# Attention followed by a spectral mix on one core: the mode weights loaded by transfers of four modes instead of two, into tiles of eight modes instead of four

## The chip, the cores and the metric

The kernel runs on one core of a Trainium2 chip; nothing else runs beside it. The metric is the device time of one launch in microseconds (us), the median of repeated runs. A core has five engines with an instruction queue each: TensorE (PE, matrix products; its weight loads are shown as PEld), VectorE (DVE), ScalarE (ACT), GpSimd (POOL) and SyncE (SP). Sixteen DMA engines move data between the device's memory (HBM) and the on-chip memory (SBUF, 128 partitions). An engine issues a transfer as an instruction of its own queue, and the transfer's landing is told by a semaphore.

## The reference, cut to what matters

```python
# batch 8, heads 8, seq 576, head_dim 64; 64 modes; d_model 512
scores = scale * q @ k.T, causal, plus a bias from the cumulated s       # softmax(scores) @ v
x = attention output as (8, 576, 512)
X = np.fft.rfft(x, axis=1)
Xr, Xi = real and imaginary part of X[:, :64]
Yr = einsum('bmd,mde->bme', Xr, w_r) - einsum('bmd,mde->bme', Xi, w_i)
Yi = einsum('bmd,mde->bme', Xr, w_i) + einsum('bmd,mde->bme', Xi, w_r)
y = np.fft.irfft(Y with the other modes zero, n=576, axis=1)
u = x + y
out = u + max(u @ w_ch, 0)
```

The weights `w_r` and `w_i` are 64 x 512 x 512 numbers of four bytes each, 67 MB apiece: every mode has its own matrix, and each is used once. They are read from HBM as float32 and written to SBUF as bfloat16, by a transfer that casts.

## The kernel before

**Stages.** The attention goes in 32 steps n = (g, b): four groups g of two heads (128 columns of d_model) times eight batches b. A step transposes q and k (`transposes`), forms the scores and their exponentials (`scores`, `scores4`), multiplies with v (`av`), and takes the forward transform of the step before (`fft`). When a group's eight batches are through, its 128 rows d of all weight matrices can be used. `modes(g, c)` does that for a chunk c of eight modes: sixteen products into one accumulator `yp`, four for each of (real or imaginary weights `ri`) times (even or odd row `q_`). Chunks of the groups 0 to 2 are spread over the steps by the table `mode_steps`; the group 3 comes after the last step, one chunk after another, between work on the output (`work`, `y_transposed`, `y_times_wch`, `gather`). After the last chunk the outputs are formed in the order of a list of steps written out by hand ("R0a X1 R0b F0a ..."): inverse transform, addition of x, product with `w_ch`, and the stores.

**Weights.** The list `wq` gives their order: group, chunk, `ri`, and half chunk `par`, 128 items in all. An item is a tile of four modes (`WM = 4`), 128 partitions x 4 x 512 bfloat16, 4 KB a partition. It is loaded by two transfers, one for each half h of the partitions: the lower 64 partitions hold the even modes of the chunk, the upper 64 the odd ones, and a partition holds two neighbouring rows d of a mode, so that one piece is 4 KB read and 2 KB written. A transfer thus has 64 partitions x 2 modes = 128 pieces, 512 KB read.

The first eight tiles lie in memory that is free until later (`y_acc` and the second half of `x_all`; the list `early`). The others take turns in two rings, `wpool` with `WA = 11` tiles and `wpool2` with `WB = 6`; from item `LW2 = 76` on only the first ring is used, because `wpool2` then holds products that are kept for the end (`first_product`, one tile for each of six pairs of output tiles). After the last weights, `wpool` holds the results on their way out (`result`, one tile for each pair).

**Order of the loads.** All of q, k, v and the weights are issued by POOL (L234, in `load`), in the order of the program: nothing overtakes. Before step n the kernel issues `load(...)` of q and k two by two, of v for step n + 3 (`LA = 3`), and of weights up to `on_chip[n]` tiles, the two lists merged evenly. `on_chip` is a plan made when the kernel is built: a share that grows step by step during the first eight steps, then three (later four) tiles a step, but no tile whose ring place is used by a chunk that has not been multiplied by then. After the last step the rest is issued in one go (L600), and each waits for its place. POOL has eight semaphores for its transfers in turn, so that a transfer waits for the landing of the eighth before it.

In the last chunk the sixteen products come in another order, since other work lies between the quarters:

```python
yb = modes(NG - 1, NCK - 1, {2: lambda: (first_z(0), first_z(1)), 3: first_u})
```

so that its four quarters use `ri` 0 `par` 0, `ri` 0 `par` 1, `ri` 1 `par` 0 and `ri` 1 `par` 1 in turn.

Of the kernel before, what the change touches and what calls it, by code (L numbers as in the profile page):

```python
# [11 lines left out]
BF16 = mybir.dt.bfloat16  # L12
# [6 lines left out]
def kernel(  # L19
# [12 lines left out]
    B, H, S, D = q.shape  # L32
    NM = moe_w_r.shape[0]
    DM = H * D
    P = 128
# [4 lines left out]
    NG = DM // P  # L40
# [5 lines left out]
    MC = 8  # L46
    NCK = NM // MC
    WM = 4
    WA, WB = 11, 6
    LA = 3  # L50
    NF = NT - 1
    RP = P // 4
# [6 lines left out]
    HP = P // 2  # L59
# [41 lines left out]
    y_acc = gp.tile([P, NCK, DM], FP32, name="y_acc")  # L101
# [7 lines left out]
    wpool = ctx.enter_context(tc.tile_pool(name="w_sb", bufs=WA))  # L109
    wpool2 = ctx.enter_context(tc.tile_pool(name="w2_sb", bufs=WB))  # L110
# [77 lines left out]

    wq = [
        (g, c, ri, par) for g in range(NG) for c in range(NCK) for ri in range(2) for par in range(2)
    ]
    early = [y_acc[:, c : c + 2, :].rearrange("p c e -> p (c e)").bitcast(BF16) for c in (2, 4, 6)]
    xg = x_all[:, NG // 2 :].rearrange("p g b t d -> p (g b t d)").bitcast(BF16)
    early += [xg[:, i * WM * DM : (i + 1) * WM * DM] for i in range(5)]
    early = [e.rearrange("p (m e) -> p m e", e=DM) for e in early]
    NE = len(early)
    wt = {}

    LW2 = 76

    def ring_of(k):
        if k < NE:
            return None
        return int(k < LW2 and (k - NE) % (WA + WB) >= WA)

    def loads_w(upto):
        todo = []
        while len(wt) < min(upto, len(wq)):  # L210
            g, c, ri, par = key = wq[len(wt)]
            i = ring_of(len(wt))
            if i is None:
                t = early[len(wt)]
            else:
                t = (wpool, wpool2)[i].tile([P, WM, DM], BF16, name="w_sb", tag="w")
            src = (moe_w_r, moe_w_i)[ri]
            m0 = c * MC + par * MC // 2
            for h in range(2):
                first = 1 if ri == 1 and m0 + h == 0 else 0  # L220
                todo.append((
                    t[HP * h : HP * h + HP, 2 * first :].rearrange("p (m q) e -> p m (q e)", q=2),
                    src[m0 + h + 2 * first : m0 + MC // 2 : 2, g * P : (g + 1) * P, :].rearrange(
                        "m (p q) e -> p m (q e)", q=2
                    ),
                ))
            wt[key] = t
        return todo

    def load(*lists):  # L230

        todo = [((i + 0.5) / len(l), x) for l in lists for i, x in enumerate(l)]
        for _, (dst, src) in sorted(todo, key=lambda t: t[0]):
            nc.gpsimd.dma_start(out=dst, in_=src)  # L234

    NW = 2 * MC // WM
    mode_steps = {B: [0, 1, 2, 3], B + 1: [4], B + 2: [5], B + 4: [6], B + 6: [7]}
    for c in range(NCK, (NG - 1) * NCK):  # L240
        mode_steps.setdefault(B + c - (0 < c % NCK < 4), []).append(c)
    used = [NW * sum(len(cs) for t, cs in mode_steps.items() if t < n) for n in range(N + 1)]
    W0 = 3
    on_chip = []
    for n in range(N):
        w = W0 + (WA + WB + NE - W0) * (n + 1) // (B + 1) if n < B else on_chip[-1] + (3 if n <= 2 * B else 4)

        nt, ring = 0, ([], [])
        while nt < min(w, len(wq)):
            i = ring_of(nt)  # L250
            if i is not None:
                depth = (WA, WB)[i]
                if len(ring[i]) >= depth and ring[i][-depth] >= used[n]:
                    break
                ring[i].append(nt)
            nt += 1
        on_chip.append(nt)


    nc.sync.dma_start(out=s_sb, in_=s.rearrange("b h t -> (b h) t"))  # L260
# [1 line left out]
    nc.sync.dma_start(out=negm32, in_=d_negm)  # L262
    first = loads_qk(0)
    load(first[:2])
    load(loads_w(W0), loads_v(0) + loads_tails(0) + first[2:] + loads_v(1))
# [189 lines left out]
    def modes(g, c, meanwhile=None):  # L455


        ps = auxpool.tile([P, DM], FP32, name="yp", tag="aux")
        cols = xs[g % 2].rearrange("p q k h r b m -> p q k (h r b) m")

        def product(ri, q_, cg):
            k0 = HP if ri == 1 and c == 0 and cg == 0 else 0
            nc.tensor.matmul(  # L463
                ps[32 * cg : 32 * cg + 32, :],
                cols[k0:, q_, 1 - ri, :, c * MC // 2 + cg],
                wt[(g, c, ri, cg // 2)][k0:, 2 * (cg % 2) + q_, :],
                start=(ri == 0 and q_ == 0), stop=(ri == 1 and q_ == 1),
                tile_position=(k0, 32 * cg), skip_group_check=True,
            )
# [59 lines left out]
    def first_transposed(i, x):  # L529
# [7 lines left out]
        xts1[i, x] = spool.tile([P, DT, P], FP16, name="xt1", tag="yt")  # L537
        nc.vector.tensor_copy(out=xts1[i, x], in_=ps)  # L538

    def first_product(i, x):  # L540
        if x == 0:
            t = wpool2.tile([P, WM, DM], BF16, name="z1", tag="w").rearrange("p m e -> p (m e)")
            kept_place(i, t)
        ps = auxpool.tile([P, DM], FP32, name="z1_ps", tag="aux")
        for dt in range(DT):
            nc.tensor.matmul(  # L546
                ps, xts1[i, x][:, dt, :], wch_sb[:, dt, :], start=(dt == 0), stop=(dt == DT - 1)
            )
        keep_product(i, x, ps)
# [7 lines left out]
    with tc.tile_pool(name="sc_psum", bufs=2, space=PSUM) as scpool, \  # L557
# [7 lines left out]
        for n in range(N):  # L565
# [21 lines left out]
            i = first_pairs[n - N + len(first_pairs)] if n >= N - len(first_pairs) else None  # L587
# [9 lines left out]
                first_product(i, 1)  # L597
        av(N - 1, 1)
        fft(N - 1)
    load(loads_w(len(wq)))  # L600
    at.close()


# [20 lines left out]
    places = [finpool.tile([P, 4 * DM], BF16, name="r_sb", tag="r", bufs=3) for i in range(2)]  # L624
# [35 lines left out]
    def keep(i):  # L660
        x_times_wch(i, True)
        j = late.index(i)
        if j < len(places):
            t = places[j]
        else:
            t = wpool.tile([P, WM, DM], BF16, name="z1", tag="w").rearrange("p m e -> p (m e)")
        kept_place(i, t)
        for x in range(2):
            keep_product(i, x, zs.pop((i, x)))

# [119 lines left out]
    def result(i):  # L790
        if i == 0:
            t = finpool.tile([P, 4 * DM], BF16, name="r_sb", tag="r", bufs=3)
        else:
            t = wpool.tile([P, WM, DM], BF16, name="r_w", tag="w").rearrange("p m e -> p (m e)")
        return t.bitcast(FP32).rearrange("p (x e) -> p x e", x=2)

    def relu(i, x):
# [62 lines left out]
    c = NCK - 2  # L860
# [69 lines left out]
    for step in (  # L930
# [8 lines left out]
        i = int(step[1:].rstrip("ab"))  # L939
# [34 lines left out]
```

## Time and profile before

| | |
|---|---|
| median of three runs | 443.68 us (443.49, 443.68, 444.41) |
| span of the profiled execution, first to last instruction | 441.4 us |
| mean granted TensorE clock | 0.914 |
| PE busy | 344.0 us (78%), 4409 products |
| DVE, ACT, POOL busy | 253.2, 226.2, 241.5 us |
| DMA packets of POOL's transfers | 63408, 81.29 MB written |
| HBM read, written | 163.51 MB, 9.44 MB |

The profile records one execution on its own, whose time outside the span is not recorded; the median of the runs is 2.3 us above its span. The page of the profile gives the busy time of each engine, the span in 40 slices with the busy share of engines and DMA, the transfers by queue and by line, the chain of waits followed back from the last instruction, and the costliest groups of instructions. A group's line shows what is written from what, how often, its busy time with the mean of one, and the idle time of its engine just before with what ended it. Behind the page, the trace can be asked for a timeline of an engine, a table by stretches of time, and the record of every DMA packet (start, duration, size).

### The profile page before, as it was taken

What the parts mean: (1) busy time and instruction counts of PE and PEld (TensorE: products, weight loads), DVE (VectorE), ACT (ScalarE), POOL (GpSimd) and SP (SyncE); (2) the same over time, 40 slices, a digit from 0 to 9 for tenths busy, and PEclk for the clock granted to TensorE, in tenths of its full rate; (3) what the DMA queues carried; (4) which work ended last, traced back from release to release, by engine and by line L of the source; (5) the groups of instructions that cost most, each with busy time, mean ns of one, the idle gap of its engine ahead of it and who ended that gap; (6) DMA issues with size and microseconds to landing.
All of it is one profiled execution on the core that took longest, in us unless ns stands there. A gap on an engine that the chain in (4) does not pass through costs nothing.

```text
span 441.4 us, 10806 instructions
## 1 busy us (share of the span) xinstructions
PE 344.0 (78%) x4409; PEld 207.5 (47%) x4409; DVE 253.2 (57%) x574; ACT 226.2 (51%) x421; POOL 241.5 (55%) x381
## 2 busy tenths in 40 slices
PE   1688998898686978792956658989987887787994
PEld 1455656465354545460634325655554445442341
DVE  7766775676545546471643515766655443451795
ACT  1486788267545725571543324666650424420794
POOL 7766566565565655555655555555544444440293
PEclk9998999999969889896786967999998988998999
DMA  9999999999999999999999999999999999998498
GB/s 180 201 206 206 204 206 205 207 207 206 209 199 207 205 208 207 207 207 208 202 206 206 208 207 203 208 205 206 200 209 211 209 210 209 210 213 163 154 383 343
DMA packets 72768, 93.25 MB, mean 211 GB/s; under 512 B 29760, under 2 KB 31296, under 8 KB 72720
## 3 DMA queue, kind: packets, MB, share of 16 engines
q0 software_dynamic: 63408, 81.29, 105.0%
q1 hardware_dynamic: 9312, 11.29, 7.7%
q8 instruction: 34, 0.56, 0.5%
q14 instruction: 14, 0.11, 0.1%
HBM read 163.51 MB, written 9.44 MB: 392 GB/s over the span
## 4 chain that ended last, share of the span: by engine, by line
DMA 53%; PE 24%; DVE 12%; issue 5%; ACT 3%; POOL 2%; DVEq 0%; ACTq 0%; POOLq 0%
DMA w_sb<-in_moe_w_i_dram 31%; DMA w_sb<-in_moe_w_r_dram 20%; PE yp L463 3%; PE sc_ps L382 3%; PE z_ps L655 3%; DMA qk<-in_k_dram 2%; PE u_ps L781 2%; DVE qt L344 2%; PE sc_ps L376 2%; POOL w_sb L234 2%; PE u_ps L751 2%; DVE xs L453 2%; PE av_ps L418 2%; PE tr_ps L340 2%; DVE xt L538 1%
## 5 line engine op out<-in xcount | busy, mean ns | idle before, releaser
L390 ACT ACTIVATE p_sb<-sc_ps,cumt_sb 128x576 f16<-128x576 f32 (+1 forms) x256 | 141.9, 636 | 22.2 <-PE sc_ps L382 21.8
L234 POOL DMA_DIRECT2D w_sb<-in_moe_w_r_dram x120 | 71.1, 594 | 59.1 <-DMA w_sb<-in_moe_w_i_dram 18.1
L234 POOL DMA_DIRECT2D w_sb<-in_moe_w_i_dram x120 | 70.9, 593 | 55.0 <-DMA w_sb<-in_moe_w_i_dram 20.2
L382 PE MATMUL sc_ps<-qt,kt 128*128 128x512 bf16 (+2 forms) x384 | 78.3, 317 | 8.2 <-ACT kt L344 7.5
L344 DVE COPY qt<-tr_ps 64x576 bf16<-64x576 bf16 x64 | 47.8, 746 | 52.5 <-PE tr_ps L340 52.5
L234 POOL DMA_DIRECT2D v<-in_v_dram x72 | 52.0, 722 | 41.3 <-DMA w_sb<-in_moe_w_r_dram 10.7
L340 PE MATMUL tr_ps<-ident,qk 64*64 64x64 bf16 x1152 | 34.6, 205 | 43.9 <-DMA qk<-in_k_dram 15.0
L382 PEld LDWEIGHTS <-kt 128*128 128x128 bf16 x384 | 38.7, 106 | 37.2 <-ACT kt L344 14.7
L340 PEld LDWEIGHTS <-qk 64*64 64x64 bf16 x1152 | 26.5, 117 | 60.7 <-DVE kt L344 19.0
L376 PE MATMUL sc_ps<-negm,ident 128*128 128x256 bf16 x256 | 54.2, 297 | 0.2
L463 PE MATMUL yp<-w_sb,xs 128*32 128x512 bf16 (+1 forms) x480 | 42.0, 415 | 15.2 <-DMA w_sb<-in_moe_w_i_dram 13.6
L361 ACT ACTIVATE p<-sc_ps,cumt 128x64 f16<-128x64 f32 x32 | 10.1, 314 | 78.0 <-PE sc_ps L357 77.8
L418 PE MATMUL av_ps<-v,p_sb 128*128 128x65 f16 x1024 | 44.3, 197 | 1.2 <-DVE x_all L428 0.5
L344 ACT COPY kt<-tr_ps 64x576 bf16<-64x576 bf16 x32 | 22.9, 715 | 37.7 <-DVE qt L344 37.2
L418 PEld LDWEIGHTS <-p_sb 128*128 128x128 f16 x1024 | 37.8, 100 | 8.4 <-DVE x_all L428 3.4
L453 DVE CAST xs<-ft_ps 64x128 bf16<-64x128 f32 x128 | 36.6, 286 | 7.2 <-PE ft_ps L443 5.8
L423 DVE TENSOR_REDUCE den<-av_ps 128x5 f32<-128x10 f32 x64 | 10.8, 169 | 50.3 <-PE av_ps L418 49.3
L463 PEld LDWEIGHTS <-xs 128*32 128x32 bf16 (+1 forms) x512 | 18.9, 145 | 32.2 <-DMA w_sb<-in_moe_w_i_dram 14.0
L428 DVE TENSOR_TENSOR x_all<-av_ps,rcp 128x320 f16<-128x320 f32 x64 | 31.5, 492 | 2.2
L524 ACT COPY z<-z_ps 128x512 f32<-128x512 f32 x22 | 12.9, 586 | 26.7 <-PE z_ps L546 14.1
L443 PE MATMUL ft_ps<-Ff_sb,x_all 128*64 128x192 f16 (+1 forms) x320 | 24.1, 264 | 1.0 <-DVE x_all L428 1.0
L344 DVE COPY kt<-tr_ps 64x576 bf16<-64x576 bf16 x32 | 24.4, 762 | 0.4
(108 smaller groups left out, 432.9 us busy)
## 6 DMA issues: line engine op xcount, KB each, us to landing
w_sb<-in_moe_w_r_dram POOLq DMA_DIRECT2D x120, 256.0 KB, 8.5
w_sb<-in_moe_w_i_dram POOLq DMA_DIRECT2D x117, 256.0 KB, 9.1
out_dram<-r_w SPq DMA_DIRECT2D x16, 512.0 KB, 3.0
v<-in_v_dram POOLq DMA_DIRECT2D x72, 64.0 KB, 7.4
qk<-in_q_dram POOLq DMA_DIRECT2D x15, 288.0 KB, 8.0
qk<-in_k_dram POOLq DMA_DIRECT2D x15, 288.0 KB, 9.1
x_all<-in_moe_w_i_dram POOLq DMA_DIRECT2D x6, 256.0 KB, 7.7
y_acc<-in_moe_w_r_dram POOLq DMA_DIRECT2D x4, 256.0 KB, 7.9
```

What stands on the lines that cost most here:

```text
L234: nc.gpsimd.dma_start(out=dst, in_=src)
L340: nc.tensor.transpose(ps[rows, r, :], src[rows, r, :], ident16[rows, rows])
L344: copy(out=to[:, :, :, half * RH : half * RH + RH], in_=ps[HP * i : HP * i + HP].rearrange("d r (h p) -> d h p r", h=2),)
L376: nc.tensor.matmul(ps[:, bass.ds(w * S, W)], ident16, negm[:, bass.ts(r, W)], start=True, stop=False, skip_group_check=True,)
L382: nc.tensor.matmul(ps[:, c0 : c0 + i1 - i0], keys[:, w, r, :], qh[:, i0:i1], start=False, stop=True, skip_group_check=True,)
L390: nc.scalar.activation(out=pt[:, poff[x] : poff[x] + S - w * W], in_=ps[:, w * S : (w + 1) * S - w * W], func=ACTF.Exp, bias=cumt_sb[:, x, ...
L418: nc.tensor.matmul(ps[:, I, r : r + NCH], lhsT, rhs, start=(i == 0), stop=(i == len(todo) - 1), skip_group_check=True,)
L428: nc.vector.tensor_tensor(out=x_all[:, g, b, :, D * h : D * h + D], in0=ps[:, :, 1 : NCH], in1=rcp.unsqueeze(2).to_broadcast([P, NT, D]), ...
L443: nc.tensor.matmul(ps[HP * q_ : HP * q_ + HP].rearrange("p h f -> p (h f)"), x_all[:nT, g, b, T, q_::2], Ff_sb[:nT, T, :], start=(T == 0), ...
L453: nc.vector.tensor_copy(out=xs[g % 2][HP * h : HP * h + HP, q_, :, h, :, b, :], in_=a)
L463: nc.tensor.matmul(ps[32 * cg : 32 * cg + 32, :], cols[k0:, q_, 1 - ri, :, c * MC // 2 + cg], wt[(g, c, ri, cg // 2)][k0:, 2 * (cg % 2) + ...
L655: nc.tensor.matmul(zs[i, x], xts[i][:, x, dt, :], wch_sb[:, dt, :], start=(dt == 0), stop=(last and dt == DT - 1), skip_group_check=True,)
```

## The change

Weights are loaded by transfers of four modes a partition half (256 pieces, 1 MB read) into tiles of eight modes (`UM`, 8 KB a partition), so that a list item is now a chunk and `ri`, 64 in all. The rings have five and three such tiles (40 and 24 KB a partition, 64 KB together; before 44 and 24, 68 KB together). The first eight half tiles lie in the free memory as four units; three of these are in one piece and are loaded by two transfers, the fourth is in two places and is loaded by four. The last unit of all is also loaded by four transfers, one half chunk after the other as before. The plan still counts half tiles but deals them in twos, starts with four instead of three, and keeps an odd rest for the next step. The kept products and the results take half a tile each (`half_of`), two to a tile. The products of `modes` are the same in number, order and shape.

```diff
     WM = 4
-    WA, WB = 11, 6
+    UM = 2 * WM
+    WA, WB = 5, 3
...
-    LW2 = 76
+    LW2 = 38
...
     def loads_w(upto):
         todo = []
-        while len(wt) < min(upto, len(wq)):
-            g, c, ri, par = key = wq[len(wt)]
-            i = ring_of(len(wt))
+        while 2 * len(wt) < min(upto, 2 * len(wq)):
+            k = len(wt)
+            g, c, ri = key = wq[k]
+            i = ring_of(k)
             if i is None:
-                t = early[len(wt)]
+                halves_, t = early[k], whole[k] if k < len(whole) else None
             else:
-                t = (wpool, wpool2)[i].tile([P, WM, DM], BF16, name="w_sb", tag="w")
+                t = (wpool, wpool2)[i].tile([P, UM, DM], BF16, name="w_sb", tag="w")
+                halves_ = [t[:, x * WM : x * WM + WM] for x in range(2)]
+            if k == len(wq) - 1:
+                t = None
             src = (moe_w_r, moe_w_i)[ri]
-            m0 = c * MC + par * MC // 2
-            for h in range(2):
-                first = 1 if ri == 1 and m0 + h == 0 else 0
-                todo.append((
-                    t[HP * h : HP * h + HP, 2 * first :].rearrange("p (m q) e -> p m (q e)", q=2),
-                    src[m0 + h + 2 * first : m0 + MC // 2 : 2, g * P : (g + 1) * P, :].rearrange(
-                        "m (p q) e -> p m (q e)", q=2
-                    ),
-                ))
-            wt[key] = t
+            for m0, m1, d in [(0, MC, t)] if t is not None else [(0, WM, halves_[0]), (WM, MC, halves_[1])]:
+                for h in range(2):
+                    first = 1 if ri == 1 and c == 0 and m0 + h == 0 else 0
+                    todo.append((
+                        d[HP * h : HP * h + HP, 2 * first :].rearrange("p (m q) e -> p m (q e)", q=2),
+                        src[
+                            c * MC + m0 + h + 2 * first : c * MC + m1 : 2, g * P : (g + 1) * P, :
+                        ].rearrange("m (p q) e -> p m (q e)", q=2),
+                    ))
+            wt[key] = halves_
...
-    W0 = 3
+    W0 = 2
...
-        w = W0 + (WA + WB + NE - W0) * (n + 1) // (B + 1) if n < B else on_chip[-1] + (3 if n <= 2 * B else 4)
+        w = 4 + 2 * (WA + WB + NE - 2) * (n + 1) // (B + 1) if n < B else plan + (3 if n <= 2 * B else 4)
+        plan = w
...
-        on_chip.append(nt)
+        if nt < w // 2:
+            plan = 2 * nt + 1
+        on_chip.append(2 * nt)
...
-                wt[(g, c, ri, cg // 2)][k0:, 2 * (cg % 2) + q_, :],
+                wt[(g, c, ri)][cg // 2][k0:, 2 * (cg % 2) + q_, :],
...
+    def half_of(pool, name):
+
+        t = open_unit.pop(name, None)
+        if t is not None:
+            return t[:, HU:]
+        t = pool.tile([P, UM, DM], BF16, name=name, tag="w").rearrange("p m e -> p (m e)")
+        open_unit[name] = t
+        return t[:, :HU]
+
     def first_product(i, x):
         if x == 0:
-            t = wpool2.tile([P, WM, DM], BF16, name="z1", tag="w").rearrange("p m e -> p (m e)")
-            kept_place(i, t)
+            kept_place(i, half_of(wpool2, "z1"))
...
         if i == 0:
             t = finpool.tile([P, 4 * DM], BF16, name="r_sb", tag="r", bufs=3)
         else:
-            t = wpool.tile([P, WM, DM], BF16, name="r_w", tag="w").rearrange("p m e -> p (m e)")
+            t = half_of(wpool, "r_w")
```

The numbers of tiles on chip by the plan, counted in half tiles of four modes, before and after: at step 3 both 12, at step 8 25 and 24, at step 16 49 and 48, at step 24 81 and 80, at step 25 85 and 82, at step 26 87 and 86, at step 31 103 and 102.

More of the change, by code (lines that the diff above doesn't have):

```diff
@@ L187, in loads_tails @@
         ]
[L191 to L194, printed above, removed]
+    wq = [(g, c, ri) for g in range(NG) for c in range(NCK) for ri in range(2)]
+    ya = y_acc.rearrange("p c e -> p (c e)").bitcast(BF16)
     xg = x_all[:, NG // 2 :].rearrange("p g b t d -> p (g b t d)").bitcast(BF16)
-    early += [xg[:, i * WM * DM : (i + 1) * WM * DM] for i in range(5)]
-    early = [e.rearrange("p (m e) -> p m e", e=DM) for e in early]
+    HU = WM * DM
+    early = [[xg[:, i * HU : i * HU + HU] for i in (0, 1)], [ya[:, i * HU : i * HU + HU] for i in (1, 2)]]
+    early += [[xg[:, i * HU : i * HU + HU] for i in (2, 3)], [ya[:, 3 * HU :], xg[:, 4 * HU : 5 * HU]]]
     NE = len(early)
+    early = [[e.rearrange("p (m e) -> p m e", e=DM) for e in pair] for pair in early]
+    whole = [xg[:, : 2 * HU], ya[:, HU : 3 * HU], xg[:, 2 * HU : 4 * HU]]
+    whole = [e.rearrange("p (m e) -> p m e", e=DM) for e in whole]
     wt = {}
-    LW2 = 76
+    LW2 = 38
     def ring_of(k):
@@ L234, in load @@
             nc.gpsimd.dma_start(out=dst, in_=src)
-    NW = 2 * MC // WM
+    NW = 2
     mode_steps = {B: [0, 1, 2, 3], B + 1: [4], B + 2: [5], B + 4: [6], B + 6: [7]}
@@ L242 @@
     used = [NW * sum(len(cs) for t, cs in mode_steps.items() if t < n) for n in range(N + 1)]
-    W0 = 3
+    W0 = 2
     on_chip = []
     for n in range(N):
-        w = W0 + (WA + WB + NE - W0) * (n + 1) // (B + 1) if n < B else on_chip[-1] + (3 if n <= 2 * B else 4)
+        w = 4 + 2 * (WA + WB + NE - 2) * (n + 1) // (B + 1) if n < B else plan + (3 if n <= 2 * B else 4)
+        plan = w
         nt, ring = 0, ([], [])
-        while nt < min(w, len(wq)):
+        while nt < min(w // 2, len(wq)):
             i = ring_of(nt)
@@ L264 @@
     load(first[:2])
-    load(loads_w(W0), loads_v(0) + loads_tails(0) + first[2:] + loads_v(1))
+    load(loads_w(2 * W0), loads_v(0) + loads_tails(0) + first[2:] + loads_v(1))
     nc.sync.dma_start(out=Ff_sb, in_=d_Ff.rearrange("(T p) c -> p T c", p=P))
@@ L538, in first_transposed @@
         nc.vector.tensor_copy(out=xts1[i, x], in_=ps)
+    open_unit = {}
+    def half_of(pool, name):
[5 more added lines that the diff above has]
+        return t[:, :HU]
     def first_product(i, x):
         if x == 0:
-            t = wpool2.tile([P, WM, DM], BF16, name="z1", tag="w").rearrange("p m e -> p (m e)")
-            kept_place(i, t)
+            kept_place(i, half_of(wpool2, "z1"))
         ps = auxpool.tile([P, DM], FP32, name="z1_ps", tag="aux")
@@ L599 @@
         fft(N - 1)
-    load(loads_w(len(wq)))
+    load(loads_w(2 * len(wq)))
     at.close()
@@ L662, in keep @@
         j = late.index(i)
[L663 to L667, printed above, removed]
+        kept_place(i, places[j])
         for x in range(2):
```

## The prediction

> **What bounds the kernel now.** The page comes first: which resource is full, and what the end hangs on.
>
> ```profile
> DMA  9999999999999999999999999999999999998498
> GB/s 180 201 206 206 204 206 205 207 207 206 209 199 207 205 208 207 207 207 208 202 206 206 208 207 203 208 205 206 200 209 211 209 210 209 210 213 163 154 383 343
> ...
> q0 software_dynamic: 63408, 81.29, 105.0%
> ...
> DMA 53%; PE 24%; DVE 12%; issue 5%; ACT 3%; POOL 2%; DVEq 0%; ACTq 0%; POOLq 0%
> ...
> L234 POOL DMA_DIRECT2D w_sb<-in_moe_w_r_dram x120 | 71.1, 594 | 59.1 <-DMA w_sb<-in_moe_w_i_dram 18.1
> ```
>
> The DMA engines are full from the first slice to slice 36, where the weights end, at an almost constant 206 GB/s written (twice that read, since weights are cast to half the size). The chain runs through weight transfers for half the span. POOL, which issues them, mostly waits for landings. So the bytes in the stream set the time until the last weights land, at 407.4 us by the landing semaphores, and the output stage of some 34 us follows.
>
> Then POOL's timeline in a stretch with nothing but weights:
>
> ```profile
> 356.62 0.59 POOL L234 DMA_DIRECT2D w_sb<-in_moe_w_r_dram  x1 [0.97 <-PE xt_ps L642]
> 357.57 0.59 POOL L234 DMA_DIRECT2D w_sb<-in_moe_w_r_dram  x1 [0.35 <-DMA w_sb<-in_moe_w_r_dram]
> 359.06 0.59 POOL L234 DMA_DIRECT2D w_sb<-in_moe_w_r_dram  x1 [0.91 <-DMA w_sb<-in_moe_w_r_dram]
> 360.07 0.59 POOL L234 DMA_DIRECT2D w_sb<-in_moe_w_r_dram  x1 [0.42 <-DMA w_sb<-in_moe_w_r_dram]
> ...
> 379.11 0.59 POOL L234 DMA_DIRECT2D w_sb<-in_moe_w_r_dram  x1 [0.90 <-DMA w_sb<-in_moe_w_r_dram]
> ```
>
> Issues keep step with landings: 18 transfers from 356.62 to 379.11, 1.25 us each. The packet records say what fills that time. One transfer puts 128/16 = 8 packets of 2 KB on each DMA engine; each starts 154 ns after the one before on its engine (the commonest spacing), and behind them stands one packet of 4 bytes, the semaphore's, 21.7 ns on average (5808 of them: 363 transfers x 16). 8 x 154 + 21.7 = 1254 ns: the spacing is explained with nothing left over.
>
> Last, PE's timeline at the end of the stream:
>
> ```profile
> 395.93 1.09 PE L463 MATMUL yp<-w_sb,xs 128*32 128x512 bf16 x16
> ...
> 401.60 1.16 PE L463 MATMUL yp<-w_sb,xs 128*32 128x512 bf16 x8
> ...
> 405.42 0.65 PE L463 MATMUL yp<-w_sb,xs 128*32 128x512 bf16 x4 [0.70 <-DMA w_sb<-in_moe_w_i_dram]
> ...
> 407.47 0.65 PE L463 MATMUL yp<-w_sb,xs 128*32 128x512 bf16 x4
> ```
>
> PE meets the last tiles with 0.70 us of waiting, and the last quarter starts when PE is through with the work before it (405.42 + 0.65 + 1.4 of L781, L751, L762), as the last transfer lands (407.43). PE and DMA are level here; a gain has to move both.
>
> **The semaphore packets.** 256 weight transfers now (by the page 120 + 117 + 6 + 4 + 4 + 3 + 1 + 1). Afterwards 62 units take two and two take four: 132. So 124 go, each with 21.7 ns on every engine: 124 x 21.7 = 2.69 us off the stream. The 2 KB packets stay, 16 in a row instead of 8. From below: if the packet runs wholly beside data, nothing is saved. The stretch excludes that, for without it eight packets would take 1232 and not 1250 ns; the spacing minus 8 x 154 gives 18, or 2.2 us in all. From above: the mean spacing over 340 to 384 us is 158 ns a packet, semaphores included; if all of 8 x 4 ns went with the transfer's end, 32 ns, 4.0 us. I take 2.69, the packet's own record.
>
> [...]
>
> **What moves PE.** Up to 354.8 us PE waits for weights chunk by chunk: chunk 2 of the last group gets its last products at 354.82, its last tile landing at 354.78. By that tile 106 of the transfers are gone: 106 x 21.7 = 2.30 us earlier. From there PE works almost without a gap until 401.60, and this block moves with its start. The next-to-last quarter waits for data: 405.37 - 2.65 = 402.7; PE is there at 404.64 - 2.3 = 402.3. The last one starts at the later of 407.43 - 2.69 = 404.7 and 402.7 + 2.05 = 404.8. So the end moves by 2.3 (PE) to 2.7 (DMA); I take 2.5. The output stage is unchanged.
>
> **Does the queue stay full?** The ring loses one half tile of 17 and places come free in twos. I compared, for every load that waits for PE, the moment its place was free with the landing of the transfer before it. Before, the smallest distances are 7.3 us (q, k at 23 us) and 9.4 us (chunk 6, second half, free at 383.51, queue busy until 392.89); else above 12 near the end. Afterwards unit k of the last stage waits for unit k - 5, both halves. The tightest is unit 61 (chunk 6, `ri` 1): it needs chunk 4's first unit, free at 383.56, and the queue then has work until unit 60 has landed, 389.86 - 2.6 = 387.3. That is 3.7 us if PE did not move at all, 6.0 if it moves by 2.3. A transfer into an idle queue costs 2.95 us beyond its own moving (the first: issued 1.24, landed 4.90, moving about 0.7). So nothing runs dry; all other units have over 10 us. At step 25 the plan sends three half tiles (7.5 us) less; the queue is over 24 us ahead there (places free at 247 to 254, busy until 278). Cost nought, covered by those distances; without cover, up to 2.95 us at one place.
>
> **Edits with one answer.** POOL: 256 pieces of v take it 722 ns, so two issues of 594 become one of about 722, over 50 us less in a queue that idles for 45%: nothing. Products need both halves of a unit at once anyway (`cg // 2` runs over both within a quarter), except in the last chunk, whose last unit stays in four transfers: nothing. At the start k of step 1 stands behind one more MB (2.5 us later); PE's first steps slip, but the queue is not fed by them: nothing at the end. Results and kept products in half tiles come back ten instead of eleven later, 9 us or more after the store that frees them, against 3.0 us for a store: nothing. SP's small loads share the engines with longer runs of weights; `qt` lands after 4.8 us now in steps of about 10: nothing, or single us of PE in steps where PE has slack.
>
> **Sum.** Profiled execution 441.4 - 2.5 = 438.9 of span; the median stands 2.3 above its span, so 443.7 - 2.5 = 441.2 us. (About 0.2%, 0.9 us, can be told from no change.)
>
> **The rivals.**
> *Longer packets (slower).* A transfer now walks four modes that lie 2 MB apart instead of two. If this lengthens the 2 KB packets, the gain is gone at 154 + 2.5/2032 = 155.2 ns (32512 packets / 16 = 2032 an engine), and each further ns costs 2.0 us. Against it: the 2 MB step is in every transfer now and the packets still run at 4096 B/154 ns = 26.6 GB/s read, on all engines alike. For it: a few packets of 220 to 294 ns stand among those of 173, and the mean is 155.3 against 154, for a reason unseen. Price: at 157 ns +6.1 - 2.5 = +3.6, 447.3 us.
> [...]
> *Gain eaten in the last chunk (no change).* The last unit's halves are now parts of one tile. If PE's third quarter waits for all four transfers, that quarter and the work behind it (0.65 + 1.4) come after the last landing: 2.5 - 2.05 = 0.45 us left, 443.2 us. Against it: the two partition halves of one tile are loaded now without one waiting for the other, and pieces of `x_all` and `y_acc` are used side by side.
> *More comes off.* From 391.13 to 407.43 eleven transfers land at 1.48 us instead of 1.25, 2.5 us lost beside SP's `yv` stores. If longer runs lose less there: up to 5 us, 438.7 us. PE, level with DMA, speaks against most of it.
>
> **How the numbers follow.** The forecast has 0.72 (own range 440.4 to 441.9 by 2.2 to 2.7 with the scatter of the three runs; 439.7 by the upper bound of 4.0), more 0.06, eaten 0.09, slower 0.13. The range from 439.8 to 443.4 takes in the eaten gain and most of the bounds, and leaves out the longer packets and the full extra gain. Faster: 0.72 + 0.06 = 0.78; same 0.09; slower 0.13.
>
> **What would show it.** Right: 132 weight transfers (239 in POOL's queue instead of 363, 1984 fewer packets of 4 bytes), 2.48 us between landings of 1 MB, 2 KB packets still 154 ns apart, DMA digits at 9 until slice 36, chunk 2's last products near 352.5, the last quarter near 404.8, the stage behind it 34 us as now. Wrong: longer packets, a DMA digit below 9 before slice 36, POOL waiting for PE in the last stage with landings over 3 us apart, or the last two quarters starting together.

## The result and the profile after

The changed kernel takes 441.92 us (median of 4 runs, 441.27 to 442.63), the kernel before beside it 443.59 us (443.42 to 444.41). The ratio is 0.9957, 95% interval 0.9945 to 0.9969: by the ratio 1.9 us faster (1.4 to 2.4), by the difference of the two medians 1.7. The forecast was 441.2 us, with a range from 439.8 to 443.4. The profiled execution is the slowest of the four, 442.63 us with a span of 440.8.

First the page after: slices of the DMA engines' busy share and of GB/s written, POOL's queue, the chain, and the two groups of weight transfers.

```profile
DMA  9999999999999999999999999999999999996498
GB/s 179 205 207 204 205 206 208 207 209 207 207 204 208 210 207 209 207 209 209 204 209 209 209 208 208 207 210 206 209 211 212 212 211 211 199 218 118 160 381 341
...
q0 software_dynamic: 61424, 81.28, 104.5%
...
DMA 52%; PE 26%; DVE 14%; issue 3%; ACT 2%; POOL 2%; DVEq 0%; POOLq 0%; ACTq 0%
...
L241 POOL DMA_DIRECT2D w_sb<-in_moe_w_i_dram x62 | 38.5, 623 | 87.5 <-PE yp L473 27.5
...
L241 POOL DMA_DIRECT2D w_sb<-in_moe_w_r_dram x60 | 37.4, 623 | 53.6 <-DMA w_sb<-in_moe_w_r_dram 33.0
```

The DMA digits stay at 9 to slice 36. The bytes are the same, with 1984 fewer packets (63408 to 61424): 124 transfers on 16 engines. The mean rate in the middle slices rises by one or two GB/s. Slice 37, where the weights run out, falls from 163 to 118.

POOL's timeline in the stretch with nothing but weights (start, duration, what, and the idle time before it with what ended it):

```profile
348.58 0.61 POOL L241 DMA_DIRECT2D w_sb<-in_moe_w_r_dram  x1 [1.62 <-DMA w_sb<-in_moe_w_r_dram]
351.31 0.61 POOL L241 DMA_DIRECT2D w_sb<-in_moe_w_i_dram  x1 [2.13 <-DMA w_sb<-in_moe_w_i_dram]
353.54 0.61 POOL L241 DMA_DIRECT2D w_sb<-in_moe_w_i_dram  x1 [1.62 <-DMA w_sb<-in_moe_w_i_dram]
...
382.31 1.22 POOL L241 DMA_DIRECT2D w_sb<-in_moe_w_i_dram  x2 [13.23 <-PE yt_ps L695]
```

One transfer moves twice as much for one issue of 0.61 us. The landings that these issues follow are 2.48 to 2.49 us apart (355.74, 358.24, 360.73, 363.21 and so on), as forecast. The 13.23 us of waiting is for unit 61's place, the spot that the forecast called the tightest. Its load was issued at 382.31, and the transfer ahead of it landed at 387.98, 5.7 us later. Yet the DMA engines were not full there (stretches of 2 us: length, busy us of PE, PEld, DVE, ACT, POOL with counts, then PE's granted clock, DMA share and GB/s):

```profile
380.00:382.00 2.00, 1.20 (x20) 0.63 (x20) 0.69 (x1) 0.59 (x1) 0.00 (x0) 1.00 1.13 212
382.00:384.00 2.00, 1.27 (x12) 0.43 (x14) 0.00 (x0) 0.59 (x1) 1.69 (x3) 1.00 0.94 167
```

A landing is told when the last of the sixteen engines is through (the issue that waits for it comes 0.28 us or more behind that); the first was through with that transfer at 382.94, 5.0 us before the last, and had nothing more to do until unit 61 came. The share falls from 1.13 to 0.94, which is 2 x 0.19/1.13 = 0.3 us of the stream.

PE's work from chunk 2 of the last group to the end of the weights. First chunk 2's last products before, in the chain that ended last (start, duration):

```profile
354.82 1.07 PE yp L463 x6
```

and the timeline of the changed kernel:

```profile
353.30 0.67 PE L473 MATMUL yp<-w_sb,xs 128*32 128x512 bf16 x8 [3.61 <-DMA w_sb<-in_moe_w_i_dram]
...
393.96 0.66 PE L473 MATMUL yp<-w_sb,xs 128*32 128x512 bf16 x8 [0.30 <-DMA w_sb<-in_moe_w_i_dram]
...
399.46 1.09 PE L473 MATMUL yp<-w_sb,xs 128*32 128x512 bf16 x8 [1.57 <-DMA w_sb<-in_moe_w_r_dram]
400.48 1.03 PE L767 MATMUL z_ps<-yv,G_sb 96*128 96x512 f16 x2
...
404.14 1.07 PE L473 MATMUL yp<-w_sb,xs 128*32 128x512 bf16 x4
...
406.79 0.65 PE L473 MATMUL yp<-w_sb,xs 128*32 128x512 bf16 x4
```

Chunk 2's last products come 1.52 us earlier than before (353.30 against 354.82), not 2.30. The last weights land at 405.46, 1.97 us earlier than before (407.43), not 2.69. And the last quarter starts at 406.79, only 0.68 us earlier: it no longer meets the landing, but comes 1.33 us behind it. The groups in between take about 1.06 us where they took 0.60. The granted clock, in the same kind of lines, tells why:

```profile
395.00:400.00 5.00, 1.97 (x16) 0.78 (x16) 1.39 (x2) 0.59 (x1) 0.00 (x0) 0.88 1.12 217
400.00:405.00 5.00, 5.00 (x24) 1.16 (x16) 0.00 (x0) 0.00 (x0) 0.00 (x0) 0.50 0.66 123
```

PE runs at half its clock over 400 to 405 us. Before, the same stretch had 0.73:

```profile
400.00:405.00 5.00, 4.71 (x24) 1.40 (x23) 0.69 (x1) 0.00 (x0) 0.00 (x0) 0.73 1.08 205
```

### The profile page after: what moved, and what is told of

Its sections match the earlier page's. It is cut to its first block, busy times and chain, and to the rows that moved or that the text cites. A ratio compares the mean times of both kernels' runs of the same rounds, so it can differ in the third digit from the quotient of the medians.

```text
span 440.8 us, 10650 instructions
## 1 busy us (share of the span) xinstructions
PE 342.5 (78%) x4409; PEld 204.5 (46%) x4409; DVE 252.9 (57%) x574; ACT 226.0 (51%) x421; POOL 171.8 (39%) x257
## 3 DMA queue, kind: packets, MB, share of 16 engines
q0 software_dynamic: 61424, 81.28, 104.5%
## 4 chain that ended last, share of the span: by engine, by line
DMA 52%; PE 26%; DVE 14%; issue 3%; ACT 2%; POOL 2%; DVEq 0%; POOLq 0%; ACTq 0%
DMA w_sb<-in_moe_w_r_dram 21%; DMA w_sb<-in_moe_w_i_dram 13%; DMA qk<-in_k_dram 8%; DMA qk<-in_q_dram 6%; DMA v<-in_v_dram 4%; PE yp L473 3%; PE sc_ps L392 3%; PE z_ps L675 3%; DVE xs L463 3%; DVE qt L354 3%; PE av_ps L428 2%; PE sc_ps L386 2%; DVE x_all L438 2%; DVE xt L548 2%; PE z_ps L767 2%
## 5 line engine op out<-in xcount | busy, mean ns | idle before, releaser
L241 POOL DMA_DIRECT2D w_sb<-in_moe_w_i_dram x62 | 38.5, 623 | 87.5 <-PE yp L473 27.5
L241 POOL DMA_DIRECT2D w_sb<-in_moe_w_r_dram x60 | 37.4, 623 | 53.6 <-DMA w_sb<-in_moe_w_r_dram 33.0
L473 PEld LDWEIGHTS <-xs 128*32 128x32 bf16 (+1 forms) x512 | 17.7, 146 | 45.9 <-DMA w_sb<-in_moe_w_i_dram 25.4
L493 DVE TENSOR_TENSOR y_acc<-yp,y_acc 128x512 f32<-128x512 f32 x16 | 11.1, 692 | 29.2 <-PE yp L473 28.5
```

The costliest lines, as they stand in the source:

```text
L473: nc.tensor.matmul(ps[32 * cg : 32 * cg + 32, :], cols[k0:, q_, 1 - ri, :, c * MC // 2 + cg], wt[(g, c, ri)][cg // 2][k0:, 2 * (cg % 2) + ...
```

## The experiments

The letters of theories in an expectation stand for what that text says of them.

**The changed kernel again** (`e1_again`, no edit), as a second trace beside the others.

> The changed kernel once more, unaltered, to see what of the 1.9 us (ratio 0.9957) is steady and what is one execution's. Theory A (the stream gains 21.7 ns for each transfer that is gone; what the end keeps of it varies by execution, since the slowest of the 16 DMA engines and PE's granted clock in the last chunk decide): ratio 0.994 to 0.996, the last weight landing in this profile again 2.0 to 2.7 us before the 407.43 of the kernel before, and the last quarter's products starting at a distance from that landing which is not the 1.3 us of the first profile. Rival B (the tiles of eight modes cost PE a fixed stretch in the last chunk): the last quarter again starts 1 us or more after the last landing.

442.12 us, ratio 0.9959 (0.9946 to 0.9972). The last weights land at 405.38, the last quarter starts at 406.14. The median span is 440.35 us against 441.70 of the kernel before, 1.35 less. What lies around the span is 1.77 against 2.07 us, so 0.3 us of the gain lie outside anything that the forecast looked at.

**Tiles, rings and plan alone** (`e2_two_modes`): every unit by four transfers of two modes.

```diff
-            for m0, m1, d in [(0, MC, t)] if t is not None else [(0, WM, halves_[0]), (WM, MC, halves_[1])]:
+            for m0, m1, d in [(0, WM, halves_[0]), (WM, MC, halves_[1])]:
```

> Tiles, rings and plan of the changed kernel, but every unit loaded by four transfers of two modes (512 KB read each), 256 weight transfers instead of 132. Theory A (only the number of transfers counts): 124 x 21.7 ns = 2.7 us back on the stream, so the time of the kernel before, ratio to it 0.999 to 1.001; packets of 4 bytes again 5808. Rival C (the gain comes from the tiles, the rings or the plan, or from fewer waits of POOL): the time of the changed kernel, ratio about 0.996.

444.41 us, ratio 1.0013 (1.0000 to 1.0026). So the number of transfers is worth 444.41 - 442.12 = 2.3 us, and the tiles, rings and plan cost about 0.6 us (0 to 1.2). The last weights land at 408.62, 1.2 us later than before, with as many semaphore packets, and 3.2 us later than in `e1_again`. Of these 3.2 us e1 loses 0.7 again: its last quarter starts 0.76 us behind the landing, that of e2 0.04 us behind it:

```profile
408.66 0.65 PE L473 MATMUL yp<-w_sb,xs 128*32 128x512 bf16 x4 [0.87 <-DMA w_sb<-in_moe_w_i_dram]
```

**One ring tile less, nothing else** (`e4_ring10`, on the kernel before).

```diff
-    WA, WB = 11, 6
+    WA, WB = 10, 6
```

> The kernel before with its first ring cut from eleven tiles to ten (64 KB of rings together, as in the change), nothing else. Theory A (the queue is over 9 us ahead of every place that comes free, a tile less costs nothing): ratio 0.999 to 1.001. Rival E (the smaller ring takes part of the gain): slower by 0.3 us or more, ratio over 1.001.

444.19 us, ratio 1.0009 (0.9996 to 1.0022); the last weights land 0.45 us later (407.88). The interval takes in no change. Nor do the 0.45 us point to the ring: a profile of a kernel with the loads and all eleven tiles of the kernel before (`e9_before_awake`, below) has the last landing at 407.77. So whether the ring has a part in the 0.6 us is not shown.

**Twice as many transfers** (`e3_one_mode`): one mode each.

```diff
-            for m0, m1, d in [(0, MC, t)] if t is not None else [(0, WM, halves_[0]), (WM, MC, halves_[1])]:
+            for m0, m1, d in [(x * 2, x * 2 + 2, halves_[x // 2][:, x % 2 * 2 : x % 2 * 2 + 2]) for x in range(4)]:
...
+                    if first:
+                        continue
```

> The same tiles, rings and plan, every unit loaded by eight transfers of one mode (256 KB read each), about 508 weight transfers. Theory A: 376 more semaphore packets on each engine than in the changed kernel, 376 x 21.7 ns = 8.2 us, so 5.5 us over the kernel before: ratio 1.012. Theory D (what counts is how many bytes eight transfers in flight hold, the stream running dry when they are few): eight transfers now hold 5 us of stream, POOL stalls of 2 to 3 us and the spread between engines empty it: ratio over 1.03. Rival C (transfers cost nothing): ratio about 0.996.

488.8 us, ratio 1.1011 (1.0982 to 1.1040). The semaphore packets account for 5.5 us of this; the rest is a stream that runs dry. From its page, the share of the DMA engines, the rate and the chain, then POOL:

```profile
DMA  9999999999999999999999999999999999999298
GB/s 181 200 172 186 177 175 165 165 173 192 200 173 191 196 176 163 190 185 199 181 195 195 159 203 186 186 171 198 184 159 200 206 196 196 203 215 166 98 362 343
...
DMA 38%; PE 24%; POOL 19%; DVE 9%; issue 8%; ACT 1%; DVEq 0%; POOLq 0%; ACTq 0%
...
L243 POOL DMA_DIRECT2D w_sb<-in_moe_w_r_dram x240 | 125.2, 533 | 41.9 <-issue 16.6
```

The digits of the DMA share stay at 9 here too, at 159 to 215 GB/s. So a 9, which the prediction named as a sign, does not tell that the queue stays full; the rate does.

In all three sizes POOL has at most eight transfers in flight, and never issues one sooner than 0.28 us after the landing of the eighth before it. Eight of this size are 8 x (4 x 154 + 21.7) = 5.1 us of stream, where the changed kernel has up to 20. Besides, an issue takes 533 ns, where the engines need 638 for the transfer. POOL has moved from 2% to 19% of the chain. Which of the two, depth or issue, costs more was not taken apart.

**The rival made true** (`e5_last_whole`): the last unit too by two transfers.

```diff
-            if k == len(wq) - 1:
-                t = None
```

> The changed kernel, but its last unit too is loaded by two transfers of eight... that is four modes a partition half, one for each half, instead of four of two modes, so that the last chunk's third quarter cannot be fed before all of it has landed. The forecast (the last quarter starts when PE is through with the third, about level with the last landing): the stream ends 2 x 21.7 ns earlier, but the third quarter starts at or behind the last landing (405.4 in the changed kernel) instead of 404.1, so the last quarter starts near 407.6 and the end comes 1 to 2 us later than in the changed kernel, 443 to 444 us. The rival (the output stage hangs on something else, and the quarter's place in the order is hidden): the same time as the changed kernel, 442.0.

444.23 us, ratio 1.0009 (0.9990 to 1.0028), 2.1 us more than the changed kernel. The third quarter comes behind the last landing (405.77):

```profile
405.82 1.08 PE L471 MATMUL yp<-w_sb,xs 128*32 128x512 bf16 x4 [1.49 <-DMA w_sb<-in_moe_w_i_dram]
409.46 0.65 PE L471 MATMUL yp<-w_sb,xs 128*32 128x512 bf16 x4
```

So without the four transfers of the last unit nothing of the gain is left at the end. The size is less firm: the twelve runs scatter from 442.57 to 447.05 us, and in this profile the third quarter and the work behind it run at half the clock, 3.64 us from its start to the last quarter's.

**The last two units by four transfers** (`e6_split_two`).

```diff
-            if k == len(wq) - 1:
+            if k >= len(wq) - 2:
                 t = None
```

> The changed kernel, but the last two units instead of the last one are loaded by four transfers of two modes each. In the changed kernel PE waits 1.57 us (0.50 in the repeated run) for the whole of the last unit but one before the last chunk's first quarter. If that wait sets the last quarter's start, which stands 0.7 to 1.4 us behind the last landing, the end comes 0.5 us earlier, ratio to the kernel before 0.9948 where the changed kernel has 0.9959. If the last landing or the work between the quarters sets it, the two further transfers cost 2 x 21.7 ns and the time is that of the changed kernel within 0.1 us.

441.02 us (five of six runs between 440.96 and 441.09), ratio 0.9939 (0.9924 to 0.9955): the fastest version. The last quarter meets the landing (405.27) again, with the clock full:

```profile
402.41 0.65 PE L473 MATMUL yp<-w_sb,xs 128*32 128x512 bf16 x4 [0.23 <-DMA w_sb<-in_moe_w_i_dram]
...
405.31 0.65 PE L473 MATMUL yp<-w_sb,xs 128*32 128x512 bf16 x4 [0.85 <-DMA w_sb<-in_moe_w_i_dram]
...
395.00:400.00 5.00, 2.44 (x16) 0.92 (x16) 1.18 (x2) 0.59 (x1) 0.00 (x0) 1.00 1.09 212
400.00:405.00 5.00, 4.23 (x25) 1.51 (x23) 0.00 (x0) 0.00 (x0) 0.00 (x0) 1.00 0.50 102
```

By the ratios it gains 0.9 us on the changed kernel, where 0.5 was expected; the two intervals overlap. PE has the first eight products of the last chunk in two parts, one of them 1.9 us earlier, and 2.44 us of work between 395 and 400 instead of 1.97.

**A small load of odd rows in every step** (`e7_odd_rows`).

```diff
+    odd = ap_.tile([P, 1021], FP32, name="odd")
...
+            nc.sync.dma_start(
+                out=odd[0:33:32, :], in_=moe_w_ch.rearrange("a e -> (a e)")[: 2 * 1024].rearrange("(a e) -> a e", a=2)[:, :1021]
+            )
```

> The changed kernel with a further small load of two rows of 1021 fp32 elements in each of the 32 steps, which nothing uses. If such a row goes to few of the sixteen DMA engines and always the same, those engines get 64 further packets of 4 KB, some 154 ns each by the rate of the weight packets: 9.9 us on one engine or 4.9 on each of two, but only 0.6 us on the mean of sixteen. Theory S (a transfer lands with its slowest engine, and the slowest engine's queue sets the end of the stream): the last landing and the end come 4 to 10 us later, 446 to 452 us, and the spread between the first and the last engine of one transfer grows by as much. Theory M (the mean over the engines sets the end, fast engines wait for none): 0.6 us later, 442.7. If the rows are spread over all engines, or the queue lets a fast engine run on no further than eight transfers ahead, it lies between.

443.84 us, ratio 0.9997 (0.9986 to 1.0008), between the two theories. At 340 and 380 us the stream is 0.7 to 1.0 us behind the two profiles of the changed kernel at equal work, and the sixteen engines' landings of one transfer lie 6.4 instead of 5.0 us apart. That spread grew by 1.4 us and not by the 9.9 of one engine, so the rows did not all go to one, and this tells little. The last two experiments come back to the question, for the stores.

**PE kept awake** (`e8_pe_awake`; the kernel before likewise in `e9_before_awake`, without the first addition; with the last two units split in `e10_split_awake`, with 3 in place of 7).

```diff
+        if meanwhile:
+            for x in range(7):
+                nc.tensor.matmul(ps, ident16h, wch_sb[:, x % DT, :], start=True, stop=True)
...
+        if c == NCK:
+            for x in range(4 * DT):
+                nc.tensor.transpose(ps[:, x % DT, :], ident16h, ident16h)
...
+        if c == NCK - 2:
+            for x in range(3):
+                nc.tensor.matmul(vp, ident16h, wch_sb[:, x, :], start=True, stop=True)
```

> The changed kernel with idle time of TensorE before the last chunk filled by work that is thrown away: 16 transposes of the identity ahead of chunk 6's transposes, 3 products ahead of its product with the channel weights, 7 ahead of the last chunk's first quarter. In the changed kernel the granted clock is 0.50 from 398.9 to 405.3 us (0.50 from 397.0 to 403.4 in the repeated run), the products there take 1.06 instead of 0.60 us, and the last quarter starts 0.8 to 1.3 us behind the last landing (0.76 in the repeated run). Theory C (the clock falls because PE was idle too long, and the slow clock is what keeps the last quarter from the landing): clock 1.00 there, last quarter within 0.1 us of the last landing, the end 0.7 to 1.3 us earlier, 441.0 us, ratio 0.994, and less scatter. Rival (PE's order and waits set the last quarter, the clock falls for another reason): the same clock or the same distance, 442.1, or later by what the added work takes.

> The kernel before with the 16 transposes and 3 products of the same kind at the same places, none ahead of the last chunk. Before, the clock is 0.50 for 3 us (399.4 to 402.7) and the last quarter starts at 407.47, 0.04 us behind the last landing. Theory C: nothing is to be had there, since the landing sets the end; ratio 1.000 within 0.001. If the clock itself cost time before too, it would gain as e8_pe_awake does, 0.997.

> The changed kernel with its last two units loaded by four transfers each and the same work thrown away (3 products ahead of the last chunk instead of 7). With four transfers each alone five of six runs lay at 441.0 and one, with a lower clock, at 442.3. Theory C: all runs at 441.0, ratio 0.994; the two measures do not add, since the last landing then sets the end in both. If the waits for whole units cost time besides the clock, it is below e8_pe_awake by some tenths.

443.00 (ratio 0.9977, 0.9967 to 0.9986), 445.38 (1.0035, 1.0021 to 1.0048) and 442.64 us (0.9971, 0.9959 to 0.9982): all three slower than expected, by 1.6 to 2.0 us. PE did what was expected in all three: the clock is 1.00 over the whole last chunk and the last quarter starts 0.04 to 0.05 us behind the landing. In `e8_pe_awake` (landing 405.39):

```profile
397.98 1.67 PE L472 MATMUL yp<-wch_sb,ident16h 128*128 128x512 f16 x7
399.58 0.67 PE L476 MATMUL yp<-w_sb,xs 128*32 128x512 bf16 x8
...
405.44 0.65 PE L476 MATMUL yp<-w_sb,xs 128*32 128x512 bf16 x4 [0.88 <-DMA w_sb<-in_moe_w_i_dram]
```

There PE's last product starts 1.36 us earlier than in the changed kernel's profile (433.44 against 434.80), but the last store lands at 439.92 against 439.74. Fifteen engines are done with that store at 438.40, the sixteenth 1.52 us later. In the trace a packet of 16 KB of queue q8, "instruction" on the page, starts at 428.65 and takes 1.51 us. From the next landing on, one engine is that much behind, and it stays so: the landings that follow are 1.2 to 1.3 us apart (the two half-size stores at the end about 0.65), and at each the sixteenth engine is 1.4 to 1.7 us behind the fifteenth. In `e9_before_awake` and `e10_split_awake` such a packet comes at 433.64 and 430.21, and the sixteenth engine is 1.61 and 1.27 us late at the last store. In the changed kernel, its repeat and the kernel with the last two units split, the last such packet came at 408.7 to 410.2 us.

**The added instructions without the work, and the work without the packet's place.** `e12_code_only` is the changed kernel with 26 one-column products thrown away far ahead of the end; `e11_awake_code` is `e8_pe_awake` with 96 of them (condition `h == 0 or r == 0`).

```diff
+            if h == 0 and r == 0 and n < 26:
+                nc.tensor.matmul(ps[:, :1], ident16, negm[:, :1], start=True, stop=True)
```

> The kernel with TensorE kept awake (16 transposes and 3 + 7 products thrown away), and besides 96 products of a single column, three in each of the 32 steps, thrown away too. In the run without them the clock was 1.00 throughout and the last quarter met the landing (405.44 against 405.39), yet the time was 443.0: a 16 KB packet of an instruction queue, which came at 408.7 us in the kernel with the split units, came at 428.65, among the result's stores, and from then on the last of the sixteen engines landed each store 1.5 us behind the fifteenth (439.92 against 438.40 at the last store). These packets come every 256 of TensorE's instructions or so, and 52 more brought one into the stores. With 192 further ones ahead of it the packet should fall near 409 us again, where no store is under way. Theory S (the end waits for the engine that carried that packet): the stores' engines land together again, 441.0 to 441.4 us, ratio 0.994. Rival (the added work on TensorE itself costs the 1.5 us): 443 or more.

> The changed kernel with 26 products of a single column, one in each of the first 26 steps, thrown away: 52 instructions for TensorE as in the kernel that was kept awake, and nothing else. Theory S: the 16 KB packet comes near 429 us, one engine lands the last stores some 1.5 us behind the others, and the time is 443.5 us (ratio 0.9993) where the changed kernel has 442.0. Rival (26 small products far ahead of the end cost nothing, the packet is hidden): 442.0, ratio 0.996.

441.52 us for the first (0.9942, 0.9929 to 0.9955) and 443.37 us for the second (0.9994, 0.9985 to 1.0003). In `e11_awake_code` the packet is at 410.0 us, and the engines land the last store 0.14 us apart (15th and 16th). In `e12_code_only` it is at 429.6, and they land it 1.77 us apart (438.53 and 440.30). Nothing else is late there: the fifteenth engine is earlier than in `e1_again` (438.95). The page's groups of DMA issues (count, KB each, median us to landing) show it for the two last half-size stores. The first line is that of `e11_awake_code`, the same as in the changed kernel's profile:

```profile
out_dram<-r_w SPq DMA_DIRECT2D x2, 256.0 KB, 3.1
```

and this is `e12_code_only`:

```profile
out_dram<-r_w SPq DMA_DIRECT2D x2, 256.0 KB, 4.9
```

So 52 instructions that do next to nothing (26 products and their 26 weight loads), over 100 us ahead of the end, cost 1.3 to 1.5 us (443.37 against 442.12 and 441.92); and PE kept awake is worth some 0.6 us (442.12 to 441.52, median spans 440.35 to 439.8), though the intervals of these two ratios overlap.

## Why the prediction held, step by step

**The semaphore packets.** The mechanism is right where the stream is full. With nothing but weights moving (346 to 387 us), two transfers of 512 KB take 2 x 1.253 = 2.506 us and one of 1 MB takes 2.480 us (changed kernel), 2.484 (e1) or 2.491 (e8): 15 to 26 ns less for one transfer fewer, where the forecast took 21.7. Over the whole stream the packets are not the whole account. By the bytes that POOL's transfers have moved, the changed kernel is ahead of the kernel before by 0.25 us at 80 us, 0.92 at 170 and 1.55 at 260, and the packets saved by then come to 0.36, 0.98 and 1.57. At 340 it is ahead by 2.82 and at 380 by 3.10 (e1: 3.01 and 3.34), and the packets come to 2.19 and 2.54. What gave the rest is not shown, and one pair of profiles is a loose measure: e9, whose loads are those of the kernel before, is itself 0.25 us behind it at 80 us and 0.75 at 340. Experiment e2 against e1 prices the 124 transfers at 2.3 us of time, where 2.69 was forecast. That the two lie so close is partly luck, for at the last landing it is 3.2 us, and e1's PE loses some of it.

**"Does the queue stay full? Cost nought."** This is the term that was mis-sized: e2 puts tiles, rings and plan at about 0.6 us (0 to 1.2). The distances were about right (5.7 us at unit 61, 6.0 forecast), but they run to the landing, which is the slowest engine's, and the forecast took the sixteen engines for one. Their landings of one transfer lay 2.3 us apart before (340 to 380 us) and 5.0 to 5.1 us in the changed kernel, so that a distance of 5.7 us left the fast ones idle: 0.3 us in the profiled run, less than 0.1 in e1, where the load came 1.1 us earlier. A sign that the prediction had named for being wrong came with it: POOL waited for PE, and unit 61's first landing was 3.11 us behind the landing before it, not 2.48. Where the rest of the 0.6 us goes stays open.

**What moves PE.** Chunk 2's last products moved by 1.52 instead of 2.30 us, as the landing of its weights did (354.78 to 353.26). Here too the sixteen engines are not one: their mean at this landing moved by 2.87 us (353.52 to 350.65), more than forecast, but the slowest, for which the landing waits, stood 1.3 us behind the mean before and 2.6 in the changed kernel. Then the step failed on its own ground. "This block moves with its start" took PE's durations as fixed. They hang on the clock, which by stretches of 1 us was 0.50 from 398.8 to 405.7 us (396.9 to 403.7 in e1), against 399.2 to 402.7 before. The last quarter, forecast at 404.8, came at 406.79 and 406.14. With PE kept awake (e8) it came at 405.44, at the landing. In the first profile, part of the idle time ahead of the fall is a wait that the prediction put at nothing: the last chunk's first two quarters use the two halves of the last unit but one in turn, and now the first of them waits for the whole unit (1.57 us). In e1 it is the wait for unit 61 (2.33 us, up to 394.91). With the last unit but one loaded in four parts (e6) the clock stayed at 1.00 and the last quarter met the landing. At the last quarter's start the change brought 0.7 to 1.3 us of the 2.5 forecast.

**Sum.** The two errors in the span were partly made good by a part that was held fixed, which is luck. Outside the span 0.3 us went too (1.77 against 2.07 us), in every kernel with fewer transfers but also in e3, which has more; e2, with as many as before, has 1.92. The number of transfers does not explain it, and it stays open. Spans: -1.35; around them -0.3; together the 1.7 us of e1.

**Edits with one answer.** A weight issue takes 623 ns, where 722 was taken from v's pieces; it does not matter. The output stage behind the last quarter is 34.0 us as before.

**The rivals.** *Longer packets* is out: 32512 packets of 2 KB as before, commonest spacing 154 ns as before. *Gain eaten in the last chunk* did not come, since the third quarter starts at 404.14, before the last landing at 405.46. Made true in e5 it cost 2.1 us, near the 2.05 forecast, but not by the forecast's path: that counted 2.05 us for the third quarter and the work behind it, which took 3.64 in e5's profile, at half the clock. *More comes off* is out: the last landings beside the `yv` stores still take 1.46 us for half a MB (twelve halves from 387.98 to 405.46), against 1.48 before.

## What to carry to other kernels

Where the DMA engines were full here, a transfer fewer saved 15 to 26 ns, about its semaphore packet of 21.7 ns on each engine; halving the number of transfers brought 2.3 us of 444. Fewer, larger transfers also keep more in flight under a limit of eight (19.8 us of stream with 1 MB each, 5.1 with 256 KB). Their price is at the end, where the last tile should still come in small parts (2.1 us here). A landing waits for the slowest of the sixteen engines (5.0 us behind the first in the changed kernel), so a distance reckoned from landings can hide engines that already stand idle. A difference of one or two us can come from an edit's side: the clock of an engine that now waits elsewhere (PE's at 0.50 for 6.8 us here in place of 3.4), or a 16 KB packet of queue q8 that now falls among the last stores (1.3 to 1.5 us in e12). Both are to be looked at before a small result is put down to the edit itself.

## What the runs showed of the hardware beyond that

**PE's clock falls without a long pause.** In the traces of the two kernels (before, after) the granted clock is 1.00 or 0.50, and each stretch between two changes lasted 3.41 us or a whole multiple of that, up to 85.33. In the last chunk it was 0.50 for 3.4 us (before) or 6.8 us (after, e1). In the changed kernel no gap near the fall is longer than 1.57 us, while PE was busy for 1.43 of the 3.41 us ahead of it (1.54 before). With the work that `e8_pe_awake` adds, the clock stayed at 1.00 although PE waits 2.11 us there, up to 394.54. How much work would hold the clock up is not shown: ahead of another fall PE was busy for 2.43 of the 3.41 us (before, from 334.39); and in e6 it was busy for 1.45 us of the four from 393 to 397, and the clock stayed at 1.00.

**The slowest of sixteen engines is the one that counts.** A 16 KB packet of queue q8 took 0.89 to 1.43 us in the traces of the two kernels (34 packets in each) and 1.51 in e8. Among the last stores the engine that is behind from then on does not catch up: the last store lands 1.3 to 1.8 us late (e8, e9, e10, e12). In e9 and e12 that is more than the packet itself took (0.93 and 0.92 us), for a reason that stays open. In the traces of the two kernels such packets come 254 of PE's records apart on the mean (165 to 338), and with 52 instructions more a further one (35 in place of 34) came among the stores, at 428.65 us in e8 and 429.6 in e12. The weights can meet the same lag: in e1 such a packet starts at 389.70, and from the next landing to the last (405.38) the sixteenth engine is 1.3 to 1.8 us behind the fifteenth. The spread of 5.0 us is another matter, and its reason stays open: in the changed kernel two such packets fall into the stretch from 346 to 384 us (352.02 and 373.88), and the spread stays at 5.1.

**At most eight transfers in flight from POOL.** POOL's transfers use eight semaphores in turn (99 to 106 in the traces of the two kernels), and the next is issued 0.28 us or more after the oldest has landed, whatever the size. With 256 KB read each, eight do not keep the stream full (488.8 us, 159 to 215 GB/s). With 512 KB and with 1 MB the rate in slices 2 to 36 stays at 199 GB/s or more.
